# Attention, dense layer and routed experts on one core: the engines of the first tiles' steps are exchanged, and the start is ordered anew

## Chip, cores and metric

One core of a Trainium2 chip runs the whole program. The metric is the device time of one execution in microseconds; of several executions the median is taken.

## What is computed

The reference is a chain of three parts over 2304 tokens of width 512. The inputs of the dense layer's weights come as 64-bit floats.

```python
scores = q @ k.T / sqrt(64)                     # 4 sequences of 576 tokens, 8 heads of 64
scores = where(0 <= rel < 128, scores - slope * rel, -1e9)   # rel: distance to an earlier key
a = softmax(scores) @ v                         # x: 2304 x 512
h = x @ w_in                                    # 512 -> 2048, float64 weights
x = (s * relu(h) ** 2 + b) @ w_out              # 2048 -> 512, float64 weights
logits = x @ w_gate + log1p(exp(x @ w_noise)) * noise        # 8 experts, the best two per token
out = sum over the two of weight_e * (relu(x @ w1[e]) @ w2[e])   # 512 -> 1024 -> 512
```

## The kernel before

**Two numbers for one.** Most matmuls take their operands as a pair of fp32r numbers, a high and a low part, and add three products (high by high, high by low, low by high). The high part is a copy on ScalarE, the low part the difference (`low`, L117).

**Attention** goes in 18 tiles of 128 tokens and, in a tile, in units of two heads (`u` is 4 times the tile plus the pair). `qk` multiplies a unit's queries by its keys on TensorE into the score tiles `sp` (L302), takes the masked row minimum on VectorE (L317), the exponential with its sum on ScalarE (L319), and the reciprocal and the normalisation on VectorE (L322 to L326). `ptr` transposes the result, `av` multiplies it by the values, and `evac` writes a chunk's input as `xh` and `xl`. Tiles 0 to 4 use plain fp32 for the scores, later ones the pairs. GpSimd scales a tile's queries (`scale_q`, L274).

**The weights** of the dense layer are 32 units of 128x512 (16 MB as float64). `split_load` fetches a unit as 128x1024 words. `conv1` (ScalarE, L125) scales the upper word; `conv2` (VectorE, L130, L131, L133) puts the bits of both words together to an fp32 number; `conv3` makes the high part on ScalarE (L139) and the low part on GpSimd (`low`, L118: `wil` and `wol`). A unit's raw buffer, one of four, is free for a new load when its low part is done. Each call of `conv_step` does one of these steps for units that follow each other.

**The dense layer** goes in 9 chunks of 256 tokens: `l1` (L434, then L441 to L446 on ScalarE and VectorE) and `l2` (L477). Chunks 0 and 1 run over the weights half by half, so that a unit of weights is used soon after its conversion. A list of steps is run in between, so that attention goes ahead of the chunk that needs it (`attn_to`), and conversions go ahead of the layer by a fixed number of units (`conv_to`).

**Routing and experts** follow: gate, ranks, gathers by GpSimd, and the two matmuls of each expert.

**The order on an engine** is not that of the code. The framework's scheduler moves an instruction ahead of others where their operands allow it, and the queues are then fixed when the program is built; each engine runs its own in order.

Of the kernel before, what the change touches and what calls it, by code (L numbers as in the profile page):

```python
# [7 lines left out]
F32 = mybir.dt.float32  # L8
# [4 lines left out]
AF = mybir.ActivationFunctionType  # L13
OP = mybir.AluOpType
# [3 lines left out]
def body(tc, q, k, v, w_in, w_out, s_in, b_in, w_gate, w_noise, noise, w1, w2, out):  # L18
    nc = tc.nc
# [5 lines left out]
    NP = H // 2  # L25
# [41 lines left out]
    qs = ap.tile([128, NP, 1], F32, name="qs")  # L67
# [7 lines left out]
    tokf = cp.tile([128, NTT], F32, name="tokf")  # L75
# [41 lines left out]
    def low(eng, dl, x, dh):  # L117
        eng.tensor_tensor(out=dl, in0=x, in1=dh.bitcast(F32), op=OP.subtract)  # L118
# [3 lines left out]
    def conv1(u):  # L122
        lo, hi, dst_h, dst_l, x = u
        z = x["z"] = ap.tile([128, 512], F32, name="z", tag="ptl", bufs=2).rearrange("p (k c) -> p k c", k=lo.shape[1])
        nc.scalar.activation(z, hi.bitcast(F32), AF.Copy, scale=float(2.0 ** -112))  # L125

    def conv2(u):
        lo, hi, dst_h, dst_l, x = u
        zi = x["z"].bitcast(I32)
        nc.vector.tensor_scalar(hi, zi, 4, 1, op0=OP.logical_shift_left, op1=OP.logical_shift_right)  # L130
        nc.vector.scalar_tensor_tensor(out=hi, in0=lo, scalar=29, in1=hi, op0=OP.logical_shift_right,  # L131
                                       op1=OP.bitwise_or)
        nc.vector.scalar_tensor_tensor(out=hi, in0=zi, scalar=-0x80000000, in1=hi, op0=OP.bitwise_and,  # L133
                                       op1=OP.bitwise_or)

    def conv3(u):
        lo, hi, dst_h, dst_l, x = u
        f = hi.bitcast(F32)
        nc.scalar.activation(dst_h, f, AF.Copy)  # L139
        low(nc.gpsimd, dst_l, f, dst_h)  # L140

    units = []

# [13 lines left out]
    C0 = 1  # L157
# [5 lines left out]
    FK = 5  # L163
# [16 lines left out]
    for ti in range(NTT):  # L180
        segs, g = [], ti * 128
        while g < ti * 128 + 128:
            b, s0 = divmod(g, S)
            n = min(S - s0, ti * 128 + 128 - g)
# [21 lines left out]
    def load_rows(nm, ti):  # L206
        if ti >= NTT:
            return
        if nm == "v" and ti < FX:
            t = vblock(F32).rearrange("p (h d) -> p h d", d=D)  # L210
        else:
            t = ap.tile([128, H, D], F32, name="rows", tag="rows", bufs=3)
        if nm == "v":
            nc.sync.dma_start(t, v[ti * 128:(ti + 1) * 128, :].rearrange("p (h d) -> p h d", d=D))
        else:
            t = t.rearrange("p h d -> p (h d)").rearrange("p (a b) -> p a b", b=128)
            nc.sync.dma_start(t, {"k": k, "q": q}[nm][ti])
        rows[nm, ti] = t

    KT = []  # L220
    QT = {}

    def q_tiles(ti):
        if ti == 0 and FK:
            QT["k"] = ap.tile([128, NP, 256], F32, name="kf", tag="qd")
        if ti == FK:
            KT.extend(ap.tile([128, NP, 256], F32R, name=t, tag=t) for t in ("k0", "k1"))
            QT["d"] = ap.tile([128, NP, 2, 128], F32R, name="qd", tag="qd")
            QT["l"] = ap.tile([128, 2, 2, 128], F32R, name="ql", tag="ql")
            nc.gpsimd.memset(QT["l"].bitcast(F32), 0.0)  # L230
# [5 lines left out]
    def t_qk(ti, nm):  # L236

        c = slice(tiles[ti].so * 128, tiles[ti].so * 128 + 128)
        if nm == "k":
            r = rows.pop((nm, ti))  # L240
            if ti < FK:
                q_tiles(ti)
                nc.scalar.activation(QT["k"][:, :, c], r, AF.Copy)
                return
            old = QT.get("k")
            q_tiles(ti)
            if ti == FK and tiles[ti].prev:
                cb = slice(128 - c.start, 256 - c.start)
                split_k(old[:, :, cb], cb)
            split_k(r, c)  # L250
        elif ti < FK:
            QT["q"] = rows.pop((nm, ti))
        else:
            r, qd = rows[nm, ti], QT["d"]
            for e, h in enumerate(halves):
                nc.scalar.activation(qd[h, :, e, :], r[h], AF.Copy)
                nc.scalar.activation(qd[halves[1 - e], :, e, :], qd[h, :, e, :].bitcast(F32), AF.Copy)
            low_q(ti, 0)
# [12 lines left out]

    def scale_q(ti):
        r = rows["q", ti]
        nc.gpsimd.tensor_tensor(out=r, in0=r, in1=qs.to_broadcast([128, NP, 128]), op=OP.mult)  # L274

    def split_v(ti):
        r = rows.pop(("v", ti)).rearrange("p h d -> p (h d)")
        if ti < FX:
            V[ti] = (r, r)
        else:  # L280
            if ti == FX and tiles[ti].prev:
                halve_v(ti - 1, V[ti - 1][0])
            halve_v(ti, r)
        load_rows("v", ti + 1)

    def vblock(dt):
        return ap.tile([128, DM], dt, name="vb", tag="vb", bufs=4)

    def halve_v(ti, r):
        V[ti] = (vblock(F32R), vblock(F32R))  # L290
        nc.scalar.activation(V[ti][0], r, AF.Copy)
        low(nc.gpsimd, V[ti][1], r, V[ti][0])

    def qk(u):
        ti, p = divmod(u, NP)
        T = tiles[ti]
        c = slice(0, 256) if T.prev else slice(T.so * 128, T.so * 128 + 128)
        m = mask_of(ti)
        sp = [sps[e][:, u % 2, :] for e in range(2)]
        if ti < FK:  # L300
            for e, r in enumerate(halves):
                nc.tensor.matmul(sp[e][:, c], QT["q"][r, p, :], QT["k"][r, p, c], start=True, stop=True)  # L302
        else:
            for e in range(2):
                nc.tensor.matmul(sp[e][:, c], QT["d"][:, p, e, :], KT[e][:, p, c], start=True, stop=False)
            for e in range(2):
                nc.tensor.matmul(sp[e][:, c], QT["l"][:, p % 2, e, :], KT[e][:, p, c], start=False, stop=True)  # L307
        st = ap.tile([128, 3, 2], F32, name="st", tag="st", bufs=3)
        pt = []
        for e in range(2):  # L310
            h = 2 * p + e
            t = ap.tile([128, 256], F32, name="pr", tag="pr", bufs=4)
            to, ts, tm = t[:, c], sp[e][:, c], m[:, 128:256]
            if T.prev:
                to, ts, tm = (x.rearrange("p (a b) -> p a b", a=2) for x in (to, ts, m))
                tm = tm if T.so else tm[:, ::-1, :]
            nc.vector.tensor_tensor_reduce(out=to, in0=ts, in1=tm, scale=-float(2.0 ** -(h + 1)), scalar=3.0e38,  # L317
                                           op0=OP.add, op1=OP.min, accum_out=st[:, 0, e:e + 1])
            nc.scalar.activation(t[:, c], t[:, c], AF.Exp, bias=st[:, 0, e:e + 1], scale=-1.0,  # L319
                                 accum_out=st[:, 1, e:e + 1])  # L320
            pt.append(t)
        nc.vector.tensor_scalar(st[:, 1, :], st[:, 1, :], 1e-9, None, op0=OP.add)  # L322
        nc.vector.reciprocal(st[:, 2, :], st[:, 1, :])
        for e in range(2):
            x = pt[e][:, c]
            nc.vector.tensor_scalar(x, x, st[:, 2, e:e + 1], None, op0=OP.mult)  # L326
        P[u] = pt

    def blocks(ti):
# [50 lines left out]
    def add_t(ti):  # L380
        def f(ti=ti):
            t_qk(ti, "k")
            load_rows("k", ti + 1)
        add(f)

        def f(ti=ti):
            t_qk(ti, "q")
            if ti < FK:
                load_rows("q", ti + 1)
        add(f)  # L390

    for u in range(NU + 2):
        ti, p = divmod(u, NP)
# [123 lines left out]
    def route1(c):  # L517
        lg = LG.pop(c)
        g, n = lg[:, :, 0:E], lg[:, :, E:2 * E]
        e = small([128, 2, E], F32, "r_e")  # L520
        u = small([128, 2, E], F32, "r_u")
# [15 lines left out]
        rec = mp.tile([128, 2, 2, 2], F32, name="rec", tag="rec", bufs=3)  # L537
# [4 lines left out]
        nc.vector.reciprocal(rec[:, :, 0, 1], d[:, :, 1])  # L542
        nc.vector.tensor_tensor(out=rec[:, :, 1, 1], in0=d[:, :, 0], in1=rec[:, :, 0, 1], op=OP.mult)
        for kx in range(2):
            nc.vector.tensor_copy(rec[:, :, kx, 0], tokf[:, 2 * c:2 * c + 2])
        ef = small([128, 2, 2], F32, "r_ef")
        nc.vector.tensor_copy(ef, mi[:, :, 0:2])
        oh = small([128, 2, 2, E], F32, "r_oh")
# [1 line left out]
                                in1=ef[:, :, :, None].to_broadcast([128, 2, 2, E]), op=OP.is_equal)  # L550
# [77 lines left out]
    def idx_for(tokens):  # L628
        for i, (_, _, d) in enumerate(steps):
            if d >= tokens:  # L630
                return i + 1
        return len(steps)
# [164 lines left out]
    zeros = []  # L797


    for nm in "kqv":  # L800
        load_rows(nm, 0)
    scale_q(0)
    split_v(0)

    def conv_to(n):
        while cst[0] < min(n, len(units) + LD + 3):
            conv_step()

    n0 = idx_for(CH)
    conv_to(C0)  # L810
    for x in range(n0):
        run_to(idx=x + 1)
        conv_to(C0 + (x + 1) * N0 // n0)
# [20 lines left out]
    for gi in range(len(pairs) + 1):  # L834
        if zeros:
            nc.sync.dma_start(*zeros.pop(0))
        if gi < len(pairs):
            c, i = pairs[gi]
# [10 lines left out]
        for z in range(4):  # L849
            if z < 2 and gi < len(pairs):  # L850
                c, i = pairs[gi]
# [4 lines left out]
            if z >= 2 and gi > 0:  # L856
                c, i = pairs[gi - 1]
# [68 lines left out]
    with tc.If(over > SL):  # L926
# [11 lines left out]
        with tc.For_i(0, E) as e:  # L938
# [4 lines left out]
            with tc.For_i(CT, NTT) as j:  # L943
# [12 lines left out]
                for f in range(KF):  # L956
# [3 lines left out]
                    out=out, out_offset=bass.IndirectOffsetOnAxis(ap=fi[:, 0:1], axis=0),  # L960
# [44 lines left out]
```

## Time and profile before

| | before |
|---|---|
| median of 3 runs | 1128.32 us (1128.16 to 1128.74) |
| the profiled execution | 1122.95 us |
| its span, first to last instruction | 1121.3 us |
| TensorE busy | 1064.5 us, 95% |
| VectorE, ScalarE, GpSimd busy | 603.8, 530.6 and 330.0 us |
| mean granted clock of TensorE | 0.987 |
| DMA | 100.16 MB, mean 89 GB/s |

PE is TensorE's matmuls and PEld its weight loads, DVE is VectorE, ACT ScalarE, POOL GpSimd, SP the queue that issues most DMAs. Busy times count an instruction from its recorded start to its end. A TensorE that waits inside a group of matmuls can still be shown as busy, so the number of matmuls in a stretch tells more than the busy share.

### The profile page before, as it was taken

To read this page: it belongs to the slowest core of one execution; us is meant where nothing else is said; L and a number is where in the kernel's file an instruction comes from. 1 tells how busy PE (TensorE), PEld (TensorE's weight loads), DVE (VectorE), ACT (ScalarE), POOL (GpSimd) and SP (SyncE) were. 2 spreads that over 40 slices of the span, in tenths; PEclk is the share of its full clock that TensorE was granted. 3 is DMA by queue.
4 is the path that set the end of the run, shared out by engine and by line. 5 is a ranking of instruction groups with operands and counts; after the bars stand their busy time and mean duration, and the time that the engine had idled before them with its cause. 6 is when DMAs were issued, how large, how long until landed. Compare 5 with 4: busy or idle time off the path is not lost. (4 is left out here: it accounts for less than half of the span.)

```text
span 1121.3 us, 16787 instructions
## 1 busy us (share of the span) xinstructions
PE 1064.5 (95%) x6219; PEld 915.1 (82%) x6219; DVE 603.8 (54%) x1523; ACT 530.6 (47%) x1058; POOL 330.0 (29%) x294
## 2 busy tenths in 40 slices
PE   4887899999999999999999989999999999999996
PEld 2666788899899999999998877878887888888875
DVE  5999958775667575766555335443150421505140
ACT  5866656566555666665453135353242421524241
POOL 4244433443413233242201224232304032040213
PEclk9998999999999999999999999999999999999999
DMA  6874421111101100101051236454345443454212
GB/s 202 255 224 153 156 81 30 48 30 48 39 29 29 48 29 27 41 25 34 1 188 59 82 88 199 125 145 107 87 122 93 117 111 73 122 93 135 48 13 37
DMA packets 53011, 100.16 MB, mean 89 GB/s; under 512 B 12340, under 2 KB 22712, under 8 KB 52920
## 3 DMA queue, kind: packets, MB, share of 16 engines
q1 hardware_dynamic: 41016, 76.87, 22.0%
q0 software_dynamic: 11904, 22.08, 10.5%
q8 instruction: 57, 0.93, 0.3%
q14 instruction: 34, 0.28, 0.1%
HBM read 78.28 MB, written 23.78 MB: 91 GB/s over the span
## 5 line engine op out<-in xcount | busy, mean ns | idle before, releaser
L434 PE MATMUL hp<-xh,wih 128*128 128x256 f32 x576 | 169.6, 295 | 2.5 <-ACT wih L139 2.2
L434 PE MATMUL hp<-xl,wih 128*128 128x256 f32 x576 | 165.0, 286 | 2.5 <-DVE xl L118 2.5
L434 PE MATMUL hp<-xh,wil 128*128 128x256 f32 x576 | 164.8, 286 | 2.5 <-POOL wil L118 2.5
L760 PE MATMUL ys<-woh,wih 128*128 128x512 f32 x512 | 160.3, 394 | 1.7 <-ACT yo L776 1.4
L692 POOL DMA_INDIRECT xg<-x2d,ix x48 | 47.7, 993 | 314.5 <-PE xp L57 274.7
L477 PE MATMUL o<-woh,gh 128*128 128x512 f32 x288 | 118.1, 410 | 3.4 <-ACT gh L445 3.4
L477 PE MATMUL o<-woh,gl 128*128 128x512 f32 x288 | 116.0, 403 | 5.1 <-DVE gl L446 5.1
L776 ACT ACTIVATE yo<-ys,ls 128x512 f32<-128x512 f32 x48 | 32.4, 688 | 180.6 <-issue 147.5
L434 PEld LDWEIGHTS hp<-xh,wih 128*128 128x128 f32 x576 | 111.0, 193 | 7.1 <-ACT wih L139 3.1
L434 PEld LDWEIGHTS hp<-xl,wih 128*128 128x128 f32 x576 | 111.4, 193 | 5.6 <-DVE xl L118 4.3
L434 PEld LDWEIGHTS hp<-xh,wil 128*128 128x128 f32 x576 | 111.2, 193 | 3.6 <-POOL wil L118 3.5
L477 PE MATMUL o<-wol,gh 128*128 128x512 f32 x288 | 114.1, 396 | 0.0
L760 PEld LDWEIGHTS ys<-woh,wih 128*128 128x128 f32 x512 | 95.1, 188 | 20.9 <-ACT yo L776 1.8
L715 PE MATMUL hp<-xh,wih 128*128 128x512 f32 (+1 forms) x288 | 107.1, 372 | 3.1 <-DVE wil L708 2.5
L715 PE MATMUL hp<-xl,wih 128*128 128x512 f32 (+1 forms) x288 | 106.8, 371 | 2.2 <-PEq L741 0.9
L715 PE MATMUL hp<-xh,wil 128*128 128x512 f32 (+1 forms) x288 | 105.9, 368 | 1.0 <-PEq L741 0.4
L118 POOL TENSOR_TENSOR ql<-rows,qd 64x256 fp32r<-64x256 f32 x52 | 39.1, 752 | 210.8 <-PE sp L307 141.6
L760 PE MATMUL ys<-woh,wil 128*128 128x512 f32 x256 | 100.1, 392 | 0.3 <-PEq L772 0.2
L777 POOL DMA_INDIRECT out_dram<-yo,ix x48 | 79.9, 1666 | 69.0 <-ACT yo L776 55.0
L707 ACT ACTIVATE wih<-hp 128x512 fp32r<-128x512 f32 x64 | 37.9, 593 | 102.4 <-PE hp L715 102.2
L319 ACT ACTIVATE pr<-pr,st 128x256 f32<-128x256 f32 (+1 forms) x144 | 70.3, 489 | 32.3 <-DVE st L317 30.2
L708 DVE SCALAR_TENSOR_TENSOR wil<-hp,wih 128x512 fp32r<-128x512 f32 x64 | 44.1, 689 | 71.9 <-ACT wih L707 71.9
(179 smaller groups left out, 2311.5 us busy)
## 6 DMA issues: line engine op xcount, KB each, us to landing
raw<-in_moe_w_dram SPq DMA_DIRECT2D x64, 512.0 KB, 4.1
w<-in_moe_w_in_dram SPq DMA_DIRECT2D x16, 512.0 KB, 3.6
w<-in_moe_w_out_dram SPq DMA_DIRECT2D x16, 512.0 KB, 3.8
x2d<-x SPq DMA_DIRECT2D x22, 256.0 KB
rows<-in_k_dram SPq DMA_DIRECT2D x18, 256.0 KB, 2.7
rows<-in_q_dram SPq DMA_DIRECT2D x18, 256.0 KB, 2.6
out_dram<-zero SPq DMA_DIRECT2D x18, 256.0 KB, 4.3
rows<-in_v_dram SPq DMA_DIRECT2D x14, 256.0 KB, 4.1
```

The costliest lines, as they stand in the source:

```text
L118: eng.tensor_tensor(out=dl, in0=x, in1=dh.bitcast(F32), op=OP.subtract)
L319: nc.scalar.activation(t[:, c], t[:, c], AF.Exp, bias=st[:, 0, e:e + 1], scale=-1.0, accum_out=st[:, 1, e:e + 1])
L434: nc.tensor.matmul(h[:, fi, :], a[:, kk, fs], bb[:, kk, cs], start=m == 0, stop=m == 3 * KD - 1)
L477: nc.tensor.matmul(o, a[:, ts], bb[:, f, :], start=i == i0 and m == 0, stop=i == i1 and m == 5)
L692: nc.gpsimd.indirect_dma_start(out=x, out_offset=None, in_=x2d, in_offset=bass.IndirectOffsetOnAxis(ap=LS[e, j][1], axis=0))
L707: nc.scalar.activation(dh, p, AF.Relu)
L708: nc.vector.scalar_tensor_tensor(out=dl, in0=p, scalar=0.0, in1=dh.bitcast(F32), op0=OP.max, op1=OP.subtract)
L715: nc.tensor.matmul(o, a[:, kk, fs], xt(z, c0, c1)[:, kk, :], start=m == 0, stop=m == 3 * KD - 1)
L760: nc.tensor.matmul(o, ht(z, j * 128, j * 128 + 128)[:, f // 2, f % 2], b[:, f, :], start=m == 0, stop=m == 3 * KF - 1)
L776: nc.scalar.activation(yo, y, AF.Copy, scale=wt)
L777: st = nc.gpsimd.indirect_dma_start(out=out, out_offset=bass.IndirectOffsetOnAxis(ap=ix, axis=0), in_=yo, in_offset=None, bounds_check=NT ...
```

## The change

- The low parts of the 32 weight units move from GpSimd to VectorE.
- The normalisation of tiles 2, 3 and 4 moves from VectorE to ScalarE.
- `after` ties an instruction behind another on the same engine, without a semaphore. The first conversion's `conv1` is tied behind the second exponential of unit 0, `conv2` behind the scores of unit 1, and the copies of token numbers in `route1` behind the scores of unit 32, each only where that unit is already in the table when the line is run.
- The keys of tiles 0 and 1 are loaded straight to their place in `kf`, in pieces of 128 numbers, and ScalarE's copy of them is dropped.
- The first tile's queries are scaled in four pieces; at the start the first weights are loaded ahead of the values.

```diff
 def conv1(u):
-        nc.scalar.activation(z, hi.bitcast(F32), AF.Copy, scale=float(2.0 ** -112))
+        after(nc.scalar.activation(z, hi.bitcast(F32), AF.Copy, scale=float(2.0 ** -112)), "x")
 def conv2(u):
-        nc.vector.tensor_scalar(hi, zi, 4, 1, op0=OP.logical_shift_left, op1=OP.logical_shift_right)
+        after(nc.vector.tensor_scalar(hi, zi, 4, 1, op0=OP.logical_shift_left, op1=OP.logical_shift_right), 1)
 def conv3(u):
-        low(nc.gpsimd, dst_l, f, dst_h)
+        low(nc.vector, dst_l, f, dst_h)
+    SCORED = {}
+    def after(ins, u):
+        if u in SCORED:
+            tc.add_manual_dep(ins.ins, SCORED[u].ins.name,
+                              mybir.DependencyInfo(mybir.DependencyClass.NoSync, mybir.DependencyReason.DATA),
+                              reason="issue order")
 def load_rows(nm, ti):
+        if nm == "k" and ti < 2:
+            q_tiles(ti)
+            nc.sync.dma_start(QT["k"][:, :, ti * 128:ti * 128 + 128], k[ti])
+            return
 def q_tiles(ti):
-        if ti == 0 and FK:
+        if "k" not in QT and ti < FK:
 def t_qk(ti, nm):
         if nm == "k":
+            if ti < 2:
+                return
 def scale_q(ti):
-        nc.gpsimd.tensor_tensor(out=r, in0=r, in1=qs.to_broadcast([128, NP, 128]), op=OP.mult)
+        n = 1 if ti == 0 else NP
+        for p in range(0, NP, n):
+            nc.gpsimd.tensor_tensor(out=r[:, p:p + n], in0=r[:, p:p + n],
+                                    in1=qs[:, p:p + n].to_broadcast([128, n, 128]), op=OP.mult)
 def qk(u):
-            nc.vector.tensor_tensor_reduce(out=to, ...
+            SCORED[u] = nc.vector.tensor_tensor_reduce(out=to, ...
-            nc.scalar.activation(t[:, c], t[:, c], AF.Exp, ...
+            x_ = nc.scalar.activation(t[:, c], t[:, c], AF.Exp, ...
+            SCORED.setdefault("x" if e else "x0", x_)
         for e in range(2):
             x = pt[e][:, c]
-            nc.vector.tensor_scalar(x, x, st[:, 2, e:e + 1], None, op0=OP.mult)
+            if 2 <= ti < FK:
+                nc.scalar.activation(x, x, AF.Copy, scale=st[:, 2, e:e + 1])
+            else:
+                nc.vector.tensor_scalar(x, x, st[:, 2, e:e + 1], None, op0=OP.mult)
 def add_t(ti):
-            load_rows("k", ti + 1)
+            if ti:
+                load_rows("k", ti + 1)
 def route1(c):
-            nc.vector.tensor_copy(rec[:, :, kx, 0], tokf[:, 2 * c:2 * c + 2])
+            after(nc.vector.tensor_copy(rec[:, :, kx, 0], tokf[:, 2 * c:2 * c + 2]), 2 * NP * NP)
 start of the main program
-    for nm in "kqv":
-        load_rows(nm, 0)
-    scale_q(0)
-    split_v(0)
+    for nm in "kq":
+        load_rows(nm, 0)
+    conv_to(C0)
+    load_rows("k", 1)
+    load_rows("v", 0)
+    scale_q(0)
+    split_v(0)
     n0 = idx_for(CH)
-    conv_to(C0)
     for x in range(n0):
```


**VectorE at the start.** `w_130` before and `w_125` after are the raw words of the first weight unit, `sp` the scores, `pr` and `st` the exponentials and their sums. Before:

```order
L572 MEMSET r_cor 128x8
L130 TENSOR_SCALAR w_130<-z 128x512
L131 SCALAR_TENSOR_TENSOR w_130<-w_130 128x512
L545 COPY rec<-tokf 128x2 x2
L133 SCALAR_TENSOR_TENSOR w_130<-z,w_130 128x512
L317 ISA pr,st<-sp_119,base 128x128
L317 ISA st 128x1
L317 ISA pr,st<-sp_120,base 128x128
L317 ISA st 128x1
L317 ISA pr,st<-sp_119,base 128x128
L317 ISA st 128x1
```

After:

```order
L595 MEMSET r_cor 128x8
L568 COPY rec<-tokf 128x2 x2
L335 ISA pr,st<-sp_119,base 128x128
L335 ISA st 128x1
L335 ISA pr,st<-sp_120,base 128x128
L335 ISA st 128x1
L335 ISA pr,st<-sp_119,base 128x128
L335 ISA st 128x1
L341 TENSOR_SCALAR st<-st 128x2
L335 ISA pr,st<-sp_120,base 128x128
L335 ISA st 128x1
L342 RECIPROCAL st<-st 128x2
```

The first unit's conversion stood ahead of all scores; now the first two units' scores and the sum of the first stand ahead of it. The two copies `rec<-tokf` stood inside the conversion and now stand ahead of the first scores.

**VectorE in the middle of the conversions**, one unit of the layer after another (`g`, `gl` belong to the layer's first matmul). Before:

```order
L442 SCALAR_TENSOR_TENSOR g<-hp,g 128x512
L130 TENSOR_SCALAR w_1039<-z 128x512
L131 SCALAR_TENSOR_TENSOR w_1039<-w_1039 128x512
L446 SCALAR_TENSOR_TENSOR gl<-g,sb_c,gh 128x512
L133 SCALAR_TENSOR_TENSOR w_1039<-z,w_1039 128x512
L130 TENSOR_SCALAR w_1079<-z 128x512
L131 SCALAR_TENSOR_TENSOR w_1079<-w_1079 128x512
L133 SCALAR_TENSOR_TENSOR w_1079<-z,w_1079 128x512
L442 SCALAR_TENSOR_TENSOR g<-hp,g 128x512
L130 TENSOR_SCALAR w_1101<-z 128x512
```

After:

```order
L465 SCALAR_TENSOR_TENSOR g<-hp,g 128x512
L133 SCALAR_TENSOR_TENSOR w_864<-z,w_864 128x512
L118 TENSOR_TENSOR wol<-w_855,woh 128x512
L469 SCALAR_TENSOR_TENSOR gl<-g,sb_c,gh 128x512
L130 TENSOR_SCALAR w_974<-z 128x512
L130 TENSOR_SCALAR w_1016<-z 128x512
L131 SCALAR_TENSOR_TENSOR w_974<-w_974 128x512
L118 TENSOR_TENSOR wol<-w_864,woh 128x512
L465 SCALAR_TENSOR_TENSOR g<-hp,g 128x512
L133 SCALAR_TENSOR_TENSOR w_974<-z,w_974 128x512
```

Per weight unit VectorE had three instructions; now it has four, the low part behind the high part of ScalarE, and an instruction or two of the next unit mostly stand in between.

**ScalarE at tile 2.** `pth` is a transposed block, `z`, `wih` and `woh` belong to conversions. Before:

```order
L344 ACTIVATE pth<-tp 128x512
L125 ACTIVATE z<-w_371 128x512
L139 ACTIVATE wih<-w_285 128x2x256
L319 ACTIVATE pr,st<-pr,st 128x256 x2
L344 ACTIVATE pth<-tp 128x512
L125 ACTIVATE z<-w_409 128x512
L319 ACTIVATE pr,st<-pr,st 128x256 x2
```

After:

```order
L366 ACTIVATE pth<-tp 128x512
L139 ACTIVATE woh<-w_243 128x512
L337 ACTIVATE pr,st<-pr,st 128x256 x2
L366 ACTIVATE pth<-tp 128x512
L139 ACTIVATE wih<-w_284 128x2x256
L346 ACTIVATE pr<-pr,st 128x256 x2
L337 ACTIVATE pr,st<-pr,st 128x256 x2
L391 ACTIVATE xh<-av 64x2x128 x2
```

The normalisation `pr<-pr,st` without a sum as output (L346) is new on ScalarE; it stands behind a transposed block's copy and a high part.

## Rows read from the trace of the kernel before

**Rows 1.** Windows of the first 500 us: stretch, its length, busy us (instructions) per engine.

```profile
core 0: us, PE busy (x) PEld busy (x) DVE busy (x) ACT busy (x) POOL busy (x), PEclk, DMA share, GB/s
0.00:10.00 10.00, 0.80 (x4) 0.51 (x4) 2.09 (x15) 3.17 (x4) 3.77 (x14) 1.00 0.75 262
10.00:40.00 30.00, 22.43 (x75) 13.12 (x76) 23.39 (x90) 20.15 (x58) 9.86 (x12) 0.94 0.74 208
40.00:143.00 103.00, 86.25 (x459) 69.27 (x458) 100.32 (x186) 68.08 (x141) 47.42 (x34) 0.91 0.60 184
143.00:160.00 17.00, 17.00 (x115) 15.43 (x114) 7.66 (x18) 6.77 (x13) 5.49 (x4) 0.97 0.22 71
...
200.00:500.00 300.00, 297.68 (x2084) 274.48 (x2083) 202.48 (x660) 178.72 (x403) 100.37 (x102) 1.00 0.12 35
```

**Rows 2.** Groups, VectorE, 0 to 150 us: busy us, mean ns of one.

```profile
L131 DVE SCALAR_TENSOR_TENSOR w<-w 128x512 int32<-128x512 int32 x32 | 31.1, 971 | 0.3
L133 DVE SCALAR_TENSOR_TENSOR w<-z,w 128x512 int32<-128x512 int32 x32 | 29.9, 936 | 0.3
L130 DVE TENSOR_SCALAR w<-z 128x512 int32<-128x512 int32 x32 | 18.9, 594 | 7.7 <-ACT z L125 6.6 <-issue 1.0
L326 DVE TENSOR_SCALAR pr<-pr,st 128x256 f32<-128x256 f32 x28 | 12.1, 472 | 0.1
L446 DVE SCALAR_TENSOR_TENSOR gl<-g,sb_c,gh 128x512 fp32r<-128x512 f32 x11 | 11.2, 1018 | 0.8 <-ACT gh L445 0.8
```

**Rows 3.** Timeline near 120 us, VectorE and GpSimd: start, duration, instruction.

```profile
119.61 0.74 DVE L446 SCALAR_TENSOR_TENSOR gl<-g,sb_c,gh 128x512 fp32r<-128x512 f32 x1
...
120.27 0.68 DVE L133 SCALAR_TENSOR_TENSOR w<-z,w 128x512 int32<-128x512 int32 x1
...
120.88 0.42 DVE L130 TENSOR_SCALAR w<-z 128x512 int32<-128x512 int32 x1
...
121.33 0.70 DVE L131 SCALAR_TENSOR_TENSOR w<-w 128x512 int32<-128x512 int32 x1
...
122.36 1.77 POOL L118 TENSOR_TENSOR wil<-w,wih 128x512 fp32r<-128x512 f32 x1 [3.22 <-DVE w L130]
...
122.87 1.81 DVE L131 SCALAR_TENSOR_TENSOR w<-w 128x512 int32<-128x512 int32 x1
...
125.21 1.21 DVE L133 SCALAR_TENSOR_TENSOR w<-z,w 128x512 int32<-128x512 int32 x1
```

**Rows 4.** Timeline at 30 us, VectorE: two normalisations, the time of both.

```profile
30.18 0.59 DVE L326 TENSOR_SCALAR pr<-pr,st 128x256 f32<-128x256 f32 x2
```

**Rows 5.** Groups, GpSimd, 0 to 150 us: the weights' low parts.

```profile
L118 POOL TENSOR_TENSOR wil<-w,wih 128x512 fp32r<-128x512 f32 x16 | 23.4, 1462 | 36.0 <-ACT wih L139 21.2 <-DMA out_dram<-zero 7.2 <-DVE w L130 7.1
L118 POOL TENSOR_TENSOR wol<-w,woh 128x512 fp32r<-128x512 f32 x16 | 22.7, 1422 | 33.7 <-ACT woh L139 31.6 <-DVE w L133 1.9
```

**Rows 6.** Timeline of the first 12 us: start, duration, engine, instruction, [idle before].

```profile
5.35 0.80 PE L302 MATMUL sp<-kf,rows 64*128 64x128 f32 x4 [5.35 <-POOL rows L274]
7.98 0.66 ACT L125 ACTIVATE z<-w 128x512 f32<-128x512 f32 x1 [3.78 <-DMA w<-in_moe_w_in_dram]
...
8.68 0.43 DVE L130 TENSOR_SCALAR w<-z 128x512 int32<-128x512 int32 x1 [6.64 <-ACT z L125]
...
9.75 1.07 DVE L545 COPY rec<-tokf 128x2 f32<-128x2 f32 x2
...
11.55 0.28 DVE L317 CUSTOM_DVE_ANT_0 pr<-sp,base 128x128 f32<-128x128 f32 x1
```

**Rows 7.** Groups, VectorE, 540 to 1121 us: a subtraction of the same size.

```profile
L666 DVE TENSOR_TENSOR xl<-xp,xh 128x512 fp32r<-128x512 f32 x32 | 20.9, 687 | 59.4 <-ACT xh L665 55.2 <-ACT yo L776 4.0
```

**Rows 8.** Groups, ScalarE, 0 to 150 us: a copy of 128x256.

```profile
L344 ACT ACTIVATE pth<-tp 128x256 f32<-128x256 f32 x4 | 1.5, 378 | 0.8 <-PE tp L57 0.6
```

**Rows 9.** DMA issues of the page: KB each, median us from issue to landing.

```profile
rows<-in_q_dram SPq DMA_DIRECT2D x18, 256.0 KB, 2.6
out_dram<-zero SPq DMA_DIRECT2D x18, 256.0 KB, 4.3
```

More of the change, by code (lines that the diff above doesn't have):

```diff
@@ L316, in qk @@
                 tm = tm if T.so else tm[:, ::-1, :]
[L317 to L320, printed above, removed]
+            SCORED[u] = nc.vector.tensor_tensor_reduce(out=to, in0=ts, in1=tm, scale=-float(2.0 ** -(h + 1)), scalar=3.0e38,
+                                                       op0=OP.add, op1=OP.min, accum_out=st[:, 0, e:e + 1])
+            x_ = nc.scalar.activation(t[:, c], t[:, c], AF.Exp, bias=st[:, 0, e:e + 1], scale=-1.0,
+                                      accum_out=st[:, 1, e:e + 1])
+            SCORED.setdefault("x" if e else "x0", x_)
             pt.append(t)
```

## Prediction

> **What bounds the kernel now.** I read the windows of the first 500 us first [rows 1]. From 200 to 500 us TensorE is busy 297.7 of 300 us and runs 2084 matmuls, 6.9 per us: it is the bound there, and nothing in the change touches that part. From 40 to 143 us it is shown busy 86 of 103 us, but runs only 459 matmuls, 4.5 per us; it mostly waits in these. VectorE is busy 100.3 of the same 103 us, ScalarE 68.1, GpSimd 47.4, and the DMA engines have a share of 0.60. So VectorE is the bound of the stretch in which the weights are converted. At 143 us that ends: from there to 160 us VectorE is busy 7.7 of 17 us, and TensorE is back at 6.8 matmuls per us. What the change saves or costs lies ahead of 143 us, and as TensorE is the bound behind it, the end of the kernel moves by the same amount. I take no term for TensorE's clock: the granted 0.91 of the stretch falls on an engine that waits anyway.
>
> Next I read what VectorE does there [rows 2]. The three conversion steps, 32 of each, cost 971, 936 and 594 ns on average. The timeline near 120 us says what they cost by themselves: 0.70, 0.68 and 0.42 us, and the layer's `gl` 0.74 us [rows 3]. Beside a low part on GpSimd (122.36 us, 1.77 us long) the same L131 takes 1.81 us. One engine holds up the other, so a low part on GpSimd is not free for VectorE.
>
> The first 40 us are read from the timeline [rows 6] and the windows [rows 1]. TensorE has the first unit's scores at 5.35 + 0.80 = 6.15 us. VectorE takes them up at 11.55 us, since its queue has the first conversion ahead of them, and this waits for its words until 7.98 us. VectorE is idle for 7.9 us of the first 10 and 6.6 us of the next 30.
>
> **The change part by part.**
>
> *Low parts on VectorE: more work.* 32 subtractions of 128x512. The nearest row, the same form with one operand in PSUM, takes 687 ns [rows 7]. Instructions of this length follow each other closer than that, as their ends overlap: the L133 of 120.27 us, 0.68 us long, has the next behind it at 120.88 [rows 3], 0.61 us on. So they occupy 32 x 0.61 = +19.5 us; the upper bound is 32 x 0.69 = +22.0.
>
> *Low parts off GpSimd: less waiting.* What VectorE loses beside GpSimd is the mean less the time by itself: L131 32 x (971 - 700) = 8.7 us; L133 32 x (936 - 680) = 8.2; L130 32 x (594 - 420) = 5.6; L326 28 x (472 - 330) = 4.0, where 330 is the second half of a pair that takes 0.59 us with an overlap [rows 4]; L446 11 x (1018 - 740) = 3.1. Together 29.6 us. The low parts of the weights are 23.4 + 22.7 = 46.1 us [rows 5] of the 61 us that GpSimd is busy before 143 us [rows 1], or 76%; the rest scales queries and splits keys and values, and stays. I take 0.76 x 29.6 = -22.4 us. Bounds: all of it, -29.6; or the smallest delay in the rows, L133's 1.21 - 0.68 = 0.53 us, 32 times, -17.0. In the middle the low part is thus worth 0.70 us on GpSimd against 0.61 on VectorE: nearly a draw, and the sign hangs on it.
>
> *Normalisation of tiles 2 to 4 on ScalarE.* 24 instructions, of which 20 lie ahead of 143 us (28 in [rows 2], less tile 1's 8). By themselves two take 0.59 us [rows 4], so VectorE loses 20 x 0.30 = -6.0 us. ScalarE gains 20 x 0.38 = 7.6 us by a copy of this shape [rows 8] and has 35 us free in the stretch [rows 1], so it costs nothing by load; by its place it can: the transposes of a unit now wait behind a conversion's copy on ScalarE. That is in the last term.
>
> So the bound stretch loses 19.5 - 22.4 - 6.0 = -8.9 us, between -16.1 and -1.0.
>
> *The start.* Scores are taken up at once where they waited 11.55 - 6.15 = 5.4 us. Scaling the first quarter of the queries alone lets them start a little sooner; the keys' load in short pieces can take that back, as loads in pieces of 512 bytes land after 4.3 us where rows land after 2.6 [rows 9], so the first keys land at some 0.8 + 4.3 = 5.1 us, about where TensorE starts now. The conversion that stood ahead is not saved, it comes later, and what counts is VectorE's idle time of 7.9 + 6.6 = 14.5 us. I take -5.0, the 5.4 less a little, between 0 (the conversions are late by as much) and -9. The next loads of weights wait for the low part on VectorE, which now stands behind tile 1's scores; the first two buffers come free some us later. With four buffers and 32 units in 143 us a buffer turns once in 4 x 4.5 = 18 us, and the slower of the two loads of [rows 9] lands in 4.3, so I cost that at nothing; if that room is gone, it shows as ScalarE waiting for a load, in the last term.
>
> *The copies of token numbers* took 1.07 us between two steps of the first conversion [rows 6]. They now stand ahead of the first scores, where VectorE is idle: -1.0 us.
>
> *New gaps.* VectorE is 97% busy because its queue is always full. With the low part in its queue it waits for ScalarE's high part once per unit, and the rest of its work shrinks. I take +3 us, as many gaps again as the 2.7 us that it has now [rows 1]; between 0 and +8.
>
> *Sum:* -8.9 - 5.0 - 1.0 + 3.0 = -11.9 us. The profiled execution, 1122.95 us with a span of 1121.3, would take 1111.1. It stands 5.4 us below the median of the runs shown, 1128.32; I take the same step off the median: 1116.4 us.
>
> **A rule against it.** VectorE is the engine that has no time left, and the change gives it 32 instructions more. The Trainium skill, in *Perfetto Trace Analysis*, section Optimizing Scalar/DVE Operations, advises the opposite: where VectorE is saturated, move work to ScalarE or even to GpSimd; it adds that the two share an SBUF port, so that moving between them might not help. *SBUF — State Buffer*, section Who interferes with whom, says that an instruction of VectorE with two SBUF inputs is fully blocked by one of GpSimd that reads SBUF, or blocks it. The 1.81 us beside 1.77 us agree with that; by the advice alone the change would end in the first rival.
>
> **The rivals.**
>
> 1. *Slower: the relief does not come.* The delays stay because the rest of GpSimd's work (queries, keys, values) now meets a VectorE that always has an instruction with two SBUF operands, the low part among them. Then VectorE gets 22.0 us, loses 6.0, and with the start, the copies and the gaps the sum is +22 - 6 - 5 - 1 + 3 = +13: 1141 us. It decides where the relief is below 13 us, 0.41 us per low part. Against it: 0.53 is the least that the rows show, and GpSimd's busy time falls to a quarter. For it: in the first 40 us VectorE was often idle, and a delay there costs nothing now. 8%.
>
> 2. *ScalarE takes over.* Its 68 us of 103 become 76 of some 94; high part, normalisation and exponential then stand in one queue, and VectorE waits for it at each low part. At 0.25 us for each of the 32 units this takes 8 us of the gain: 1116.4 + 8 = 1124. For it: VectorE already waits for ScalarE's `z` 6.6 us [rows 2]. Against it: most of that was the first load. 15%, spread from 1121 to 1130.
>
> 3. *The start does not move.* Keys in short pieces land late, or the conversions are late by what the scores gain. Then only -8.9 - 1 + 3 = -6.9 is left: 1121.4. 15%.
>
> 4. *The start gains all its 9 us, or the relief is whole:* -9 - 16 - 1 + 3 = -23: 1105. 7%.
>
> 5. *One tie does nothing.* Chunk 0's copies are routed before unit 32 has scores, so the tie finds no entry; the order shows them early still. As VectorE waits there for TensorE anyway, that costs nothing, and it is in the forecast.
>
> **How the numbers follow.** The forecast has 55%, with 1109 to 1121 as its own range. The range reaches into cases 2 and 4, 1104 to 1127; it leaves out the slower case, the tail of case 2 and a little below, some 17%. A measurement of this kernel can tell about 0.2%, 2.3 us, from no change. Faster by more: the forecast's 55 (1 less for its tail), cases 3 and 4 with 22 less 1, and half of case 2, 8: 83%. The same: 7%, from the rest of case 2 and the tails. Slower: case 1 and the end of case 2, 10%.
>
> **What the profile after would show.** Right: the first scores on VectorE (L335) near 6 us; L131 and L133 at a mean near 750 ns instead of 950; the stretch in which VectorE is full ends near 131 us instead of 143, with TensorE at 6.8 matmuls per us behind it; GpSimd's busy time down by some 46 us; the part behind 200 us as before, only shifted. A low part at 0.7 us on VectorE, and no waits of TensorE for GpSimd. Wrong: L131 and L133 still above 900 ns, or low parts above 1 us (rival 1); VectorE idle for over 10 us in the stretch with ScalarE as the releaser, or TensorE waiting for L346 (rival 2); first scores at 8 us or later, or tile 1 no earlier (rival 3). A change of over 3 us in the distance from 200 us to the end would say that the end does not simply follow the start, and the argument would fail as a whole.

## The result and the profile after

Four runs before and four after the change, side by side: 1128.24 us before (1128.09 to 1128.74), **1108.12 us after** (1107.59 to 1111.9), a ratio of 0.9828 with an interval of 0.9806 to 0.985. The forecast was 1116.4 us within 1104 to 1127. On a second chip it was 1108.05 against 1124.53 us, 0.9839 (0.9812 to 0.9865). So the change saves 16 to 20 us where 11.9 were forecast.

Why 16 to 20: the kernel before scatters. Over its 58 runs beside the experiments it took 1120.2 to 1129.3 us, and the mean granted clock of TensorE in a run went from 0.993 to 0.981. The 14 runs with a clock of 0.981 to 0.983 average 1127.8 us, the 14 with 0.987 to 0.989 average 1122.8. The execution that the prediction rests on (0.987, 1122.95 us) is one of the quicker ones.

The page of the changed kernel begins thus:

```profile
span 1110.2 us, 16733 instructions
...
PE 1070.0 (96%) x6219; PEld 920.2 (83%) x6219; DVE 588.4 (53%) x1531; ACT 538.7 (49%) x1080; POOL 284.1 (26%) x265
```

Its profiled execution took 1111.9 us, the slowest of the four. GpSimd is busy 284.1 us, 45.9 less than before, as forecast. The windows, with the columns of [rows 1]:

```profile
core 0: us, PE busy (x) PEld busy (x) DVE busy (x) ACT busy (x) POOL busy (x), PEclk, DMA share, GB/s
0.00:10.00 10.00, 3.70 (x17) 2.58 (x18) 4.21 (x34) 3.59 (x10) 3.63 (x16) 1.00 0.75 244
10.00:40.00 30.00, 24.30 (x76) 14.06 (x76) 23.59 (x81) 18.98 (x54) 5.29 (x8) 0.94 0.88 246
40.00:126.00 86.00, 83.93 (x482) 68.37 (x481) 79.46 (x182) 71.11 (x153) 4.93 (x4) 0.98 0.65 199
126.00:143.00 17.00, 14.97 (x86) 13.18 (x84) 15.30 (x27) 11.50 (x20) 6.63 (x4) 0.90 0.33 100
143.00:160.00 17.00, 14.92 (x90) 13.04 (x88) 9.68 (x25) 8.94 (x20) 2.91 (x4) 0.90 0.26 85
...
200.00:500.00 300.00, 298.42 (x2091) 275.51 (x2090) 198.50 (x653) 178.07 (x403) 94.87 (x96) 1.00 0.12 36
```

From 40 to 126 us TensorE runs 482 matmuls in 86 us, 5.6 per us, where it ran 4.5 from 40 to 143 us [rows 1]. VectorE is busy 79.5 of the 86 us: it is not quite full any more, with 6.5 us of gaps. GpSimd is busy 4.9 us of them. VectorE's groups up to 150 us (busy us, mean ns, idle before) answer to [rows 2]:

```profile
L133 DVE SCALAR_TENSOR_TENSOR w<-z,w 128x512 int32<-128x512 int32 x32 | 24.1, 754 | 0.1
L131 DVE SCALAR_TENSOR_TENSOR w<-w 128x512 int32<-128x512 int32 x32 | 23.6, 737 | 0.1
L130 DVE TENSOR_SCALAR w<-z 128x512 int32<-128x512 int32 x32 | 13.6, 429 | 1.2 <-ACT z L125 1.0
L118 DVE TENSOR_TENSOR wol<-w,woh 128x512 fp32r<-128x512 f32 x16 | 13.2, 822 | 2.4 <-ACT woh L139 2.4
L118 DVE TENSOR_TENSOR wil<-w,wih 128x512 fp32r<-128x512 f32 x16 | 10.9, 681 | 0.5 <-ACT wih L139 0.5
L469 DVE SCALAR_TENSOR_TENSOR gl<-g,sb_c,gh 128x512 fp32r<-128x512 f32 x13 | 9.6, 736 | 0.3 <-ACT gh L468 0.3
```

The three conversion steps cost 754, 737 and 429 ns where they cost 936, 971 and 594; `gl` 736 where it cost 1018. That is nearly what they take by themselves [rows 3]. The low part is 681 and 822 ns; three long ones raise the second: 1.53 us beside a scaling of queries on GpSimd (37.08 us), and 1.77 and 0.95 us beside its splits of the keys (135.34 and 139.56 us).

The start, in the timeline (start, duration, [idle before]):

```profile
5.23 0.80 PE L320 MATMUL sp<-kf,rows 64*128 64x128 f32 x4 [5.23 <-POOL rows L291]
...
6.06 0.29 DVE L335 CUSTOM_DVE_ANT_0 pr<-sp,base 128x128 f32<-128x128 f32 x1 [3.20 <-PE sp L320]
...
7.40 0.66 ACT L125 ACTIVATE z<-w 128x512 f32<-128x512 f32 x1
...
8.39 0.42 DVE L130 TENSOR_SCALAR w<-z 128x512 int32<-128x512 int32 x1
```

VectorE takes up the first scores at 6.06 us, where it did at 11.55 [rows 6], and the first conversion step follows at 8.39 us, about where it stood. What comes much later is the end of this conversion, the high part on ScalarE and the low part. Before:

```profile
11.66 0.66 ACT L139 ACTIVATE wih<-w 128x512 fp32r<-128x512 f32 x1 [2.41 <-DVE w L133]
...
12.45 1.30 POOL L118 TENSOR_TENSOR wil<-w,wih 128x512 fp32r<-128x512 f32 x1 [0.60 <-POOL mask L199]
```

After:

```profile
20.46 0.65 ACT L139 ACTIVATE wih<-w 128x512 fp32r<-128x512 f32 x1
...
21.60 0.67 DVE L118 TENSOR_TENSOR wil<-w,wih 128x512 fp32r<-128x512 f32 x1
```

VectorE has started its last step of this conversion at 11.69 us (10.74 before). The high part then stands behind attention of the first two tiles in ScalarE's queue, and there ScalarE waits twice for a transposed block, 1.04 and 2.40 us.

How far ahead the changed kernel is at a later point is read from one instruction that comes once per chunk: the first of routing, of chunk 1. Before:

```profile
219.78 0.22 ACT L523 ACTIVATE r_e<-lg 128x16 f32<-128x16 f32 x1 [0.32 <-DVE lg L512]
```

After:

```profile
204.49 0.21 ACT L546 ACTIVATE r_e<-lg 128x16 f32<-128x16 f32 x1 [0.32 <-DVE lg L535]
```

It is 15.3 us ahead there, and 15.1 us at the last chunk's. Of this profile's lead 4 us are lost near 630 us, in windows that hold the same work in the changed kernel's two profiles; this one:

```profile
600.00:660.00 60.00, 54.76 (x334) 49.02 (x333) 18.70 (x63) 14.46 (x26) 14.78 (x14) 0.91 0.31 80
```

and a second profile of the same kernel:

```profile
600.00:660.00 60.00, 54.64 (x355) 47.98 (x354) 22.36 (x67) 17.23 (x30) 16.30 (x15) 1.00 0.33 84
```

In the first the granted clock is 0.91 there, so TensorE was at its lower level for a part of it, and runs 334 matmuls instead of 355. Before, and in the second profile, it is 1.00. The two profiled executions so differ by 11.1 us where the medians differ by 20.1: the one before is 5.3 us below its median, the one after 3.8 above its own, about the 4 us lost here.

### The profile page after: what moved, and what is told of

It reads as the page before. It is cut to its first block, busy times and chain, and to the rows that moved or that the text cites. A ratio compares the mean times of both kernels' runs of the same rounds, so it can differ in the third digit from the quotient of the medians.

```text
span 1110.2 us, 16733 instructions
## 1 busy us (share of the span) xinstructions
PE 1070.0 (96%) x6219; PEld 920.2 (83%) x6219; DVE 588.4 (53%) x1531; ACT 538.7 (49%) x1080; POOL 284.1 (26%) x265
```

## Experiments

All times are medians; a ratio is to the kernel before, run beside on the same chip (1124.5 to 1125.8 us there), with its 95% interval. One hundredth of it is 11.25 us. The ratio is not the quotient of the two medians, and the two can differ by some us; where that matters, both are given.

### One part alone

**Low parts on VectorE.** In the kernel before, one line:

```diff
-        low(nc.gpsimd, dst_l, f, dst_h)
+        low(nc.vector, dst_l, f, dst_h)
```

> The kernel before, with only the low parts of the weights moved from GpSimd to VectorE. My own sums (theory A) make this nearly a draw: 19.5 us of work added, 22.4 us of waiting gone, some new gaps: between -3 and +1 us, with L131 and L133 at a mean near 750 ns. Theory B, that the relief is larger than I took (a subtraction on GpSimd costs VectorE a whole blocked instruction, some 1.1 us, as soon as VectorE has no idle time): -8 us or more. Theory C, that the start carries the whole gain: 0 us.

Measured: 1116.51 us, 0.9934 (0.991 to 0.9958), so -7.4 us (-4.7 to -10.1; -9.2 by medians). A's -3 to +1 and C's 0 lie outside; B's -8 or more is inside. VectorE's groups up to 150 us:

```profile
L133 DVE SCALAR_TENSOR_TENSOR w<-z,w 128x512 int32<-128x512 int32 x32 | 25.5, 798 | 0.0
L131 DVE SCALAR_TENSOR_TENSOR w<-w 128x512 int32<-128x512 int32 x32 | 23.0, 720 | 0.0
L130 DVE TENSOR_SCALAR w<-z 128x512 int32<-128x512 int32 x32 | 14.5, 457 | 7.4 <-ACT z L125 7.4
L118 DVE TENSOR_TENSOR wol<-w,woh 128x512 fp32r<-128x512 f32 x16 | 11.1, 696 | 1.3 <-ACT woh L139 1.1
L118 DVE TENSOR_TENSOR wil<-w,wih 128x512 fp32r<-128x512 f32 x16 | 11.0, 686 | 3.0 <-ACT wih L139 3.0
```

All three steps are near their own time already with this part alone, so the waiting that the prediction put down to GpSimd's low parts is theirs. The reason that B gave, 1.1 us for each, is tried below.

**Normalisation on ScalarE**, in the kernel before:

```diff
-            nc.vector.tensor_scalar(x, x, st[:, 2, e:e + 1], None, op0=OP.mult)
+            if 2 <= ti < FK:
+                nc.scalar.activation(x, x, AF.Copy, scale=st[:, 2, e:e + 1])
+            else:
+                nc.vector.tensor_scalar(x, x, st[:, 2, e:e + 1], None, op0=OP.mult)
```

> The kernel before, with only the normalisation of tiles 2, 3 and 4 moved from VectorE to ScalarE. Theory A: -6.0 us, what VectorE loses of work in its full stretch. Theory B: -6 to -9, as these instructions also wait for GpSimd (472 ns on average against 300). Theory C: 0.

Measured: 1120.67 us, 0.9958 (0.9941 to 0.9976), -4.7 us. A's -6.0 is inside the interval (-2.7 to -6.6), as is the near end of B's range.

**The start alone.** The changed kernel with the two pieces above undone.

> The changed kernel with the low parts back on GpSimd and all normalisations back on VectorE: the reordered start alone (keys loaded to their place, queries scaled in pieces, first weights loaded ahead of the values, the ties). Theory A: -6 us, from the start and the two copies; the lead of about 5 us at the first scores is still there when the conversions end. Theory B: -3 or less, since the lead shrinks to 3 us by tile 3 as the conversions are late. Theory C: -15 us or more.

Measured: 1124.75 us, 0.9997 (0.9978 to 1.0016): nothing, or at most 2.5 us. B is right, A and C are not. The first scores of tile 2 on VectorE, in this kernel and in the one before:

```profile
38.79 0.42 DVE L335 CUSTOM_DVE_ANT_1 pr<-sp,base 128x256 f32<-128x256 f32 x1
```

```profile
39.39 0.43 DVE L317 CUSTOM_DVE_ANT_1 pr<-sp,base 128x256 f32<-128x256 f32 x1
```

At the first scores the lead was 5.4 us (6.18 against 11.55); here it is 0.6. The first low part is late in this kernel, too (21.31 us against 12.45), and chunk 1's routing starts at 221.83 us, 2 us later than in the kernel before. And as GpSimd still makes the low parts, VectorE is held up as ever (mean ns in this kernel, up to 150 us):

```profile
L133 DVE SCALAR_TENSOR_TENSOR w<-z,w 128x512 int32<-128x512 int32 x32 | 32.0, 1001 | 0.1
...
L348 DVE TENSOR_SCALAR pr<-pr,st 128x256 f32<-128x256 f32 x28 | 13.0, 504 | 0.0
```

### One part taken away

**Both moves, old start**: the two diffs above in the kernel before.

> The kernel before with the low parts on VectorE and the normalisation of tiles 2 to 4 on ScalarE, but the start as it was. Alone they gave -7.4 and -4.7 us, and the start alone 0. Theory A, each part is worth the same in company: -12 us against the kernel before (1113 to 1116 us), and some 7 us of the whole change stay unexplained. Theory D, the start is worth nothing alone because VectorE, slowed by GpSimd, eats its lead before 40 us, and it is worth 5 to 8 us once that is gone: this kernel is 5 to 8 us slower than the whole change. Theory E, the two moves help each other (the shorter VectorE queue lets ScalarE's normalisations through): this kernel is within 2 us of the whole change.

Measured: 1107.68 us, 0.9848 (0.9819 to 0.9876). The whole change, run beside it, took 1108.05 us, 0.9839. So the start is worth nothing that these runs can tell in company either; D falls, and E's number holds. Its reason, the shorter queue, was not tried. A's sum of the single parts, -12.1 us, is 5 us short of the -17.1 measured (by medians -14.3 and -16.9, 2.5 us). In this kernel's profile chunk 1's routing starts 2.2 us sooner than in the changed kernel's (204.49 us):

```profile
202.33 0.21 ACT L526 ACTIVATE r_e<-lg 128x16 f32<-128x16 f32 x1 [0.32 <-DVE lg L515]
```

**Low parts back on GpSimd**:

> The changed kernel with the low parts back on GpSimd. Theory A: -5 us against the kernel before (norms -4.7, start 0). Theory D: also -5, as the start needs the low parts off GpSimd; 13 to 15 us slower than the whole change. Theory E: -5 or less.

Measured: 1120.25 us, 0.9961 (0.9943 to 0.998), -4.4 us: what the normalisations give alone.

**Normalisations back on VectorE**:

> The changed kernel with all normalisations back on VectorE. Theory A: -7.5 us against the kernel before (the low parts alone), 12 us slower than the whole change. Theory D: low parts and start together give -13 to -15, 5 us slower than the whole change. Theory E: -8, as without the normalisations on ScalarE nothing more is won.

Measured: 1116.5 us, 0.9909 (0.9883 to 0.9935), -10.2 us (-7.3 to -13.2; -8.0 by medians). Low parts and start gave -7.4 and -0.3 alone. The interval holds A's and E's numbers and touches D's, so it says little about the start.

**The change once more**:

> The changed kernel once more, as the measure for the three beside it on the same chip. All theories: 1108 us, a ratio to the kernel before of 0.983 within 0.002; in the profile the lead over the kernel before at 200 us is 15 to 20 us.

Measured: 1108.05 us, 0.9839 (0.9812 to 0.9865). Chunk 1's routing starts at 204.35 us in it, within 0.2 us of the first profile.

Taken together, the start is worth 0.0003, -0.0003, 0.0025 and 0.0009 of the time in the four pairs with and without it: 1 us on average, each pair uncertain by 2 to 4 us. In two of the pairs, those with the low parts on VectorE, the new start also goes with a lower mean granted clock of TensorE (0.991 against 0.996, 0.989 against 0.992), and in the other two with a higher one, so what it would be worth at an equal clock stays open. The low parts are worth 7.4 us alone and 12.4 to 13.7 beside the normalisations, these 4.7 alone and 7.9 to 9.7 beside the low parts: together 4 to 5 us more than apart by ratios, 2.5 to 5 by medians. Four kernels' intervals of some 2 to 3 us each enter into that, so it is at the edge of what these runs can tell, and no run shows a reason for it.

### What a low part costs, measured

**GpSimd makes it once more** beside VectorE's. The added result is read by nobody.

```diff
         low(nc.vector, dst_l, f, dst_h)
+        low(nc.gpsimd, lo.bitcast(F32), f, dst_h)
```

> The changed kernel, and beside VectorE's low part GpSimd does the same subtraction again, into raw words that are not needed any more; nothing reads its result, only the raw buffer is free later. This measures what a subtraction on GpSimd costs VectorE. Theory A (0.70 us each, 32 of them): +22 us less what falls on idle time, so +12 to +20 against the changed kernel, 1120 to 1128 us. Theory B (1.1 us each): +25 us or more, 1133 us or more. If GpSimd's work costs VectorE nothing, as rival 1 has it, the time stays at 1108 us, and L131 and L133 stay near 750 ns.

Measured: 1131.64 us, 1.006 (1.004 to 1.008): 23.6 us above the whole change by medians, 24.9 by ratios, 0.74 to 0.78 us for each of the 32 subtractions. The ratios are the better measure, as this kernel ran on another chip than the repeated whole change. The time lies between A's and B's numbers, nearer to A's 0.70 each than to B's 1.1. So GpSimd's work is not free for VectorE. VectorE's groups up to 160 us:

```profile
L133 DVE SCALAR_TENSOR_TENSOR w<-z,w 128x512 int32<-128x512 int32 x31 | 25.5, 821 | 0.1
L131 DVE SCALAR_TENSOR_TENSOR w<-w 128x512 int32<-128x512 int32 x32 | 24.9, 777 | 0.1
L118 DVE TENSOR_TENSOR wil<-w,wih 128x512 fp32r<-128x512 f32 x16 | 21.5, 1346 | 0.0
L130 DVE TENSOR_SCALAR w<-z 128x512 int32<-128x512 int32 x32 | 20.1, 635 | 0.4 <-ACT z L125 0.3
L118 DVE TENSOR_TENSOR wol<-w,woh 128x512 fp32r<-128x512 f32 x14 | 18.2, 1297 | 0.4 <-ACT woh L139 0.4
```

Here the delay sits on VectorE's own low part, 1.3 us instead of 0.7: both start when the same high part is done, both read two operands from SBUF, and VectorE's waits. That the raw buffer comes free later does not show as a cost: up to 160 us ScalarE waits 3.9 us for loads of weights, and 6.6 in the changed kernel, while VectorE is busy all of the time from 126 to 160 us. Before, where GpSimd's started beside whatever stood in VectorE's queue, it sat on the conversion steps.

**VectorE makes it twice**, the second time for nobody:

```diff
         low(nc.vector, dst_l, f, dst_h)
+        low(nc.vector, lo.bitcast(F32), f, dst_h)
```

> The changed kernel, and VectorE makes each low part of the weights twice, the second time into raw words that are not needed any more; nothing reads it. This measures what the added work costs, as the doubled subtraction on GpSimd measured the waiting (+23.5 us, 0.73 each). Theory A, the sum of the prediction: VectorE is full, 32 times 0.61, +19 to +20 us, 1127 to 1128 us. Theory F, the term that was too large: a part of it falls into VectorE's idle time, +10 to +16 us, 1118 to 1124 us.

Measured: 1123.65 us, 0.999 (0.9975 to 1.0006): 15.6 us above the whole change by medians, 17.0 by ratios, 0.49 to 0.53 us each. F's +10 to +16 holds by medians; by ratios the number lies between F's and A's, and with these intervals A's +19 is not excluded. Two of the groups:

```profile
L118 DVE TENSOR_TENSOR wil<-w,wih 128x512 fp32r<-128x512 f32 x16 | 11.0, 685 | 2.1 <-ACT wih L139 2.0
L118 DVE TENSOR_TENSOR w<-w,wih 128x512 f32<-128x512 f32 x15 | 10.3, 684 | 0.0
```

The instruction takes 0.68 us, as forecast, and was priced at 0.61, the distance from one instruction to the next; what it adds to the end is some 0.5. Against 19.5 us that leaves 2.5 to 3.9 us. Gaps take up only a part of it: VectorE is idle 19.1 us up to the end of its last low part here (158.2 us), and 19.6 and 20.9 us in the changed kernel's two profiles (to 140.5 and 142.2 us). The rest is not explained. TensorE's mean granted clock was lower, too, 0.985 against 0.991, and its share in the 15.6 us is not separated. With the two measurements the low parts alone come to 23.6 - 15.6 = 8.0 us, against 7.4 measured.

### Parts of the start, and one more normalisation

**Keys as rows again** (loads of the first two keys through `rows` and ScalarE's copy, the rest of the change kept; the first of four places):

```diff
-        if nm == "k" and ti < 2:
-            q_tiles(ti)
-            nc.sync.dma_start(QT["k"][:, :, ti * 128:ti * 128 + 128], k[ti])
-            return
```

> The changed kernel with the keys of tiles 0 and 1 loaded as rows and copied by ScalarE, as before; the ties, the queries in pieces and the order of the first loads stay. If the loads in short pieces are what spoils the start (they fill the DMA engines from 10 to 40 us and the second weights come late), it is 2 to 5 us faster than the changed kernel. If the start does not matter, the same within 2 us.

Measured: 1107.83 us, 0.9834 (0.9809 to 0.986), the same. The first scores come at 5.49 us, 0.6 sooner than with the short pieces, and it does not matter.

**No ties** (`if u in SCORED` made false):

> The changed kernel without the three ties: the first conversion stands ahead of the first scores on VectorE again, its low part too, so that the first scores start at 11 to 13 us instead of 6. If the lead at the first scores is worth what I took, 5 us slower than the changed kernel. If it is worth nothing, as the kernel without the new start says, the same within 2 us, and 200 us are reached at the same time.

Measured: 1110.36 us, 0.9864 (0.9838 to 0.9889), with the first scores at 11.69 us, 5.6 later. It is 2.3 us slower by medians, and chunk 1's routing starts 2.8 us later in its profile (207.19 against 204.35 us); the intervals overlap. So the ties may be worth 2 to 3 us, and more at an equal clock (0.997 here, 0.991 in the changed kernel); the 5 us that I took did not come. What the queries in pieces and the new order of the first loads do by themselves was not tried.

**Tile 1's normalisation on ScalarE, too** (`1 <= ti < FK`):

> The changed kernel with the normalisation of tile 1 on ScalarE, too: 8 more instructions of 128x256. If VectorE's work ahead of 40 us counted, -2 us; as it is idle there for some 6 us, I expect no difference within 1.5 us, or a little slower where ScalarE's queue delays tile 1.

Measured: 1106.34 us, 0.9831 (0.9809 to 0.9854): the lowest median of all, but not to be told from the whole change.

## Why the prediction was right, and where it was not

**The bound** was named rightly. Taking the normalisations off VectorE shortens the run, as does taking away what held its instructions up; work or waiting added to it lengthens the run. Behind 200 us the lead does not change but for the clock.

**Low parts off GpSimd, -22.4 us:** right. Adding them once more measured 23.6 to 24.9, and the means of the conversion steps fell to 737 to 754 ns, where "near 750" was said. The share of 76% counts low parts up to 150 us against GpSimd's work up to 143; up to 143 us they are 44.8 of the 61 us, which makes -21.7.

**Low parts on VectorE, +19.5 us:** too much. It measured 15.6 to 17. I multiplied by the distance of two instructions in a full queue; what they add to the end is 2.5 to 3.9 us less, of which gaps explain 0.5 to 1.8. "Nearly a draw" was wrong: the low parts alone are worth 7.4 us, by the two doublings 8.0.

**New gaps, +3 us:** VectorE has them (6.5 us in 86), but a cost on top is not needed: the two doubled subtractions and the single part agree without such a term. With intervals of some 3 us they cannot exclude one.

**Normalisations, -6.0 us:** -4.7 alone, -7.9 to -9.7 beside the low parts; right in size.

**The start, -5.0, and the copies, -1.0:** this step failed. The first scores did come 5.5 us sooner, as the profile was to show, and it is worth about 1 us with an uncertainty larger than that. What I wrote beside it holds: the conversion "is not saved, it comes later". I had seen the low part move behind tile 1's scores and costed that at nothing. The first low part comes 9.2 us later than before, and what it waits for is its high part in ScalarE's queue, 8.8 us later. The lead is down to 0.6 us at tile 2 in the kernel with the start alone. The changed kernel's lead over the kernel with both moves and the old start is 5.9 us at the first scores (6.06 against 11.94) and 1.5 at tile 2 (35.78 against 37.26), and at chunk 1's routing it is 2.2 us behind. The idle time of the first 40 us did not shrink enough: VectorE is busy 27.8 of them after, 25.5 before. How much of the lead the late conversions take and how much the lower clock of the first 160 us is not separated. For the keys' load I read `out_dram<-zero` [rows 9] as a load; it is a store. The keys in short pieces landed after 3.2 us, not 4.3, and the first scores wait for GpSimd's scaling of the queries (5.23 us), not for them.

**The clock, no term:** also too simple. The kernel before has a mean granted clock of TensorE of 0.986 over its runs, the changed one 0.991, both moves without the start 0.996. As a run of the kernel before is some 0.7 us longer for each 0.001 less, this goes with a few of the us that the sum lacked. To separate the clock's share from the rest was not tried.

**Where the gain shows.** I said that VectorE's full stretch would end near 131 us with TensorE at 6.8 matmuls per us behind it. It ends near 140 us instead, and from 143 to 160 us TensorE runs 5.3 per us. The gain lies inside the stretch: from 40 to 143 us TensorE runs 566 matmuls where it ran 459.

**The sum** of -11.9 us thus holds errors against each other: 5 to 6 us too much from the start and the copies, 6 to 7 too little from the work and the gaps of the low parts, 1 to 2 too little from the waiting, the rest perhaps from what the two moves give together and from the clock, neither of which is settled. The gain and the wide range, 1104 to 1127, held. 1116.4 was 8 us too high, and the forecast's own range, 1109 to 1121, just misses 1108.12. That terms wrong by 5 us and more made a sum only 8 us off is luck in part.

**The rivals.** 1 (no relief) is excluded by the conversion steps after the change, 737 and 754 ns where it asked for over 900, and by the low parts alone. 2 (ScalarE takes over) did not come: VectorE's low parts waited 2.9 us for the high parts, by the groups above. 3 (the start does not move) has its number wrong and its heart right: it moved, and its lead was gone at 200 us. 4 (all 9 us from the start, or the whole relief) has the nearest number, 1105, but neither of its conditions came: the start gave about 1 us, and the relief was some 24 of 29.6 us. Its sum also takes both gains, where its words say one or the other; that would be 1112 or 1109. 5 stands: the copies still come ahead of the first scores.

On the advice against it in the Trainium skill (*Perfetto Trace Analysis*, Optimizing Scalar/DVE Operations): moving work off a saturated VectorE to ScalarE paid here, as it says that it may; moving it off to GpSimd is what this change undid. Its remark that the two share a port, so that this might not help, agrees with 0.74 us of waiting against 0.49 us of work for each low part.

## What to carry to other kernels

Work on GpSimd beside a full VectorE had a price on VectorE here; measure it by doing the work twice, once on each engine, and compare. Two such doublings gave the sign that the sum of busy times left open: what an instruction takes, and what it adds to the end, were 0.68 and some 0.5 us. A sooner start is worth only what is left of it where the stretch ends. Here the scores came 5.5 us sooner and the first conversion's end 9 us later, and little or nothing was left; follow such work through every engine's queue, as this delay stood in ScalarE's.

## What was not expected of the hardware

The same kernel's time goes with TensorE's mean granted clock from run to run: 1120.2 us at 0.993 and 1129.05 at 0.981, with identical instructions. In the profile before, the clock fell in the conversion stretch, where TensorE works with gaps: 0.91 from 40 to 143 us and 1.00 from 200 to 500 [rows 1]. In the kernel with both moves and the old start it stayed at 1.00 up to 500 us (the last three columns are granted clock, DMA share, GB/s):

```profile
10.00:40.00 30.00, 23.51 (x79) 13.11 (x79) 23.90 (x94) 20.27 (x60) 4.83 (x8) 1.00 0.75 213
40.00:126.00 86.00, 83.49 (x485) 67.99 (x485) 81.49 (x191) 72.61 (x159) 5.52 (x4) 1.00 0.69 213
126.00:143.00 17.00, 15.33 (x92) 12.19 (x91) 15.78 (x21) 10.29 (x17) 6.39 (x4) 1.00 0.26 83
```

In the changed kernel's second profile it did not:

```profile
10.00:40.00 30.00, 23.41 (x72) 13.20 (x69) 22.84 (x76) 18.53 (x53) 4.74 (x8) 0.89 0.87 245
40.00:126.00 86.00, 83.81 (x479) 68.44 (x480) 79.69 (x183) 71.09 (x154) 4.94 (x4) 0.98 0.65 197
126.00:143.00 17.00, 14.37 (x86) 12.63 (x85) 15.17 (x24) 10.04 (x18) 6.60 (x4) 0.90 0.24 83
```

It is not the new start by itself: in the kernel with the start alone the clock was 1.00 from 10 to 40 us. Whether the changed kernel loses its few us by this, as its TensorE begins earlier and then waits, is not shown.
